# Attention and two expert stages on one core: the router's broadcast loads and the gated rows change their DMA queue

## Chip, core and metric

The kernel runs on 1 core of one Trainium2 chip. The metric is the device time of one execution in microseconds (us). The core has five engines that each run their own list of instructions in order: PE (matmul; its weight loads are listed apart as PEld), DVE (vector), ACT (scalar), POOL (GpSimd) and SP (sync), which here only issues DMAs. A DMA is issued by one engine's list and then moves data on 16 DMA engines that all lists share. An instruction that waits for a semaphore holds up what is behind it in its own list, and nothing else.

## The reference, cut to what matters

Three stages follow one another: attention in chunks, a dense expert with a clipped gate, and a mixture of 8 experts where each token goes to one expert.

```
for each chunk of 32 queries:                    # batch 4, heads 8, seq 768, head_dim 64
    k_full = [mem_k (8), k[chunk - 16 : chunk + 32 + 8]];  v_full likewise
    out = softmax(q_c @ k_full.T / 8) @ v_full
x = out as 3072 tokens x 512

h = x @ w_in                                     # 512 -> 2048
x = (h * clip(h + 3, 0, 6) / 6) @ w_out          # 2048 -> 512

xn = x / |x|;  en = expert_emb / |expert_emb|    # 8 experts
logits = xn @ en.T / tau
expert_idx = argmax(logits);  gate_w = softmax(logits)[expert_idx]
out[tokens of e] = gate_w * (relu(x @ w1[e]) @ w2[e])
```

## The kernel before

The 3072 tokens are 24 tiles of 128 tokens, in 8 blocks of 4, 2, 3, 3, 3, 3, 3 and 3 tiles. A loop over blocks `bl` does the dense expert of block `bl` and, woven in, the attention of the next block's tiles and the routing of block `bl - 1`. One loop has 16 steps `f`, one for each 128 columns of the hidden layer. In a step PE does `mm1(bl, f + 1)`, 12 matmuls to the hidden part `h` (L435); ACT and DVE make `g` from it (L450, L451) and split it into `gh` (ACT, L443) and `gl` (DVE, L446); `mm2(bl, f)` is 9 matmuls from gh and gl into `acc` (L491), two with gh ahead of one with gl for each of 3 tiles. Between the two matmul groups the step's list `slot[f]` is run: pieces of attention and routing.

Attention of one tile is six pieces in steps 5a to 5a + 5. The first, `st_t`, has DVE transpose k_t into the ring `kt` (L220) and q_t into qT (L258); `put_k` then copies borders of the ring with four or five small copies on POOL (L215, L224 to L231), which wait for the transpose on DVE. As soon as the transposes have read k_t and q_t, the next tile's loads go out on SP's queue: `load_blocks` (L145) issues 16 small loads for k_t and 16 for q_t. Piece 5 issues the loads of v (L179, and of mem_v, L189) on SP, which wait for PE to be done with the buffer (L334).

Routing of a block is done in two ways. Blocks 1 to 5 (`by_dots`) take dot products on DVE: `r_en` loads one expert's scaled embedding from the DRAM tensor `en_d`, one row of 2 KB to all 128 partitions, into `enb` (L577); `r_dot` multiplies it with a tile's x2 and sums (L583). `enb` has two buffers: `r_en(bl, 0)` and `r_en(bl, 1)` stand in slot 0, behind the first attention piece, and the load for expert e + 2 is issued behind the last tile's dot with expert e. The dots are spread over steps 1 to 10 by the numbers in `DOTS`; one of each step is put between gh and gl of `mm1`, so that `gl` stands behind it on DVE. These are the loops bl = 2 to 6, from about 226 to 737 us of the trace. At step 14 `r_gate` writes the block's rows, 512 values and the inverse of the gate's sum, to the DRAM tensor `xb` (L715), one DMA for each tile. The tile x2 is then free for the next evacuation of `acc` (`evac`, L508 on DVE and L510 on ACT, in the next loop behind its first mm1). Blocks 0, 6 and 7 are routed with matmuls and write their rows in the same `r_gate`.

After the loops the expert stage (from about 745 us on) gathers rows from xb with indirect DMAs on POOL (L802, tile `xg`) and scatters its results the same way.

The order on each engine's list is that of the program: the scheduler is off, and a DMA is in the list of the engine whose name it is called on. POOL's list holds, in these loops, the copies of put_k and one small power (`root`, L604) and no DMA.

Of the kernel before, what the change touches and what calls it, by code (L numbers as in the profile page):

```python
# [17 lines left out]
P = 128  # L18
# [13 lines left out]
def attn_moe_kernel(ctx, tc, q, k, v, mem_k, mem_v, w_in, w_out, emb, tau, w1, w2, out, dbg=None):  # L32
    nc = tc.nc
    B, H, S, D = q.shape
    M = mem_k.shape[2]
    NTOK, DM = out.shape
# [71 lines left out]
    xb = dram.tile([NTOK, XW], F32, name="xb")  # L108
# [406 lines left out]
    def small(shape, dt=F32, name="small", bufs=1):  # L515
        return sb.tile(shape, dt, tag=name, name=name, bufs=bufs)
# [49 lines left out]
    en_d = dram.tile([E, DM], F32, name="en_d")  # L566
    enb = {}

    def by_dots(bl):

        return 1 <= bl <= NB - 3

    def r_en(bl, e):

        if e < E:
            enb[bl, e] = sb.tile([P, DM], F32, tag="dec", name="enb", bufs=2)
            nc.sync.dma_start(out=enb[bl, e], in_=en_d[e:e + 1, :].to_broadcast([P, DM]))  # L577

    def r_dot(bl, t, e):
        if (t, e) == (0, 0):  # L580
            blk[bl] = (small([P, BS[bl]], name="ss"), small([P, BS[bl], E], name="lg"))
        x2 = x2_t[bl, t]
        V.scalar_tensor_tensor(  # L583
            out=x2[:, XW + 1:XW + 1 + DM // 2].bitcast(BF16), in0=x2[:, 0:DM], scalar=1.0, in1=enb[bl, e],
            op0=ALU.mult, op1=ALU.mult, accum_out=blk[bl][1][:, t, e:e + 1])
        if t == BS[bl] - 1:
            r_en(bl, e + 2)
# [109 lines left out]
    def r_gate(bl):  # L697

        lg, oh = blk[bl][1:3]
        TB = BS[bl]  # L700
        for t in range(TB if bl < NB - 1 else 0):
            V.tensor_tensor(out=ocum, in0=ocum, in1=oh[:, t, :], op=ALU.add)
        sm = small([P, TB], name="r_sm")
        V.tensor_reduce(out=sm, in_=lg, axis=AX.X, op=ALU.add)
        V.tensor_scalar(out=sm, in0=sm, scalar1=1e-9, scalar2=None, op0=ALU.add)
        if bl == 0:
            V.reciprocal(out=sm, in_=sm)
            nc.sync.dma_start(out=xb[0:TB * P, DM:XW].rearrange("(t p) o -> p (t o)", p=P), in_=sm)
        for t in range(TB):
            x2 = x2_t.pop((bl, t))  # L710
            r0 = (F0[bl] + t) * P
            if bl:
                V.reciprocal(out=x2[:, DM:DM + 1], in_=sm[:, t:t + 1])
            w = XW if bl else DM
            nc.sync.dma_start(out=xb[r0:r0 + P, 0:w], in_=x2[:, 0:w])  # L715

    cnt = const.tile([1, E], F32, name="cnt")

# [274 lines left out]
    with tc.manual_schedule():  # L993
# [149 lines left out]
        for bl in range(NB):  # L1143
# [10 lines left out]
            if by_dots(bl - 1):  # L1154
                for e in range(2):
                    slot.setdefault(0, []).append(lambda e=e: r_en(bl - 1, e))
                dots = [lambda t=t, e=e: r_dot(bl - 1, t, e) for e in range(E) for t in range(BS[bl - 1])]
                for f, n in enumerate(DOTS, 1):
                    mids[f], dots = dots[:1], dots[1:]
                    slot.setdefault(f, []).extend(dots[:n])  # L1160
                    dots = dots[n:]
                for t in range(BS[bl - 1]):
                    slot.setdefault(10 + t // 2, []).append(lambda t=t: r_ss(bl - 1, t))
                for f, r_ in ((10, r_route), (11, r_rank), (12, r_sel), (13, r_list), (14, r_exp), (14, r_gate)):
                    slot.setdefault(f, []).append(lambda r_=r_: r_(bl - 1))
            else:
                d = 2 if bl == 1 else 0
                for t in range(BS[bl - 1]):
                    (wt, f), (wl, f2) = (RT4 if bl == 1 else RT)[t], (RL4 if bl == 1 else RL)[t]
                    (pre_, slot)[wt].setdefault(f, []).append(lambda t=t: r_t(bl - 1, t, spare(bl)))  # L1170
                    (pre_, slot)[wl].setdefault(f2, []).insert(0, lambda t=t: r_l(bl - 1, t))
                    slot.setdefault((8, 8, 9, 9)[t] + d // 2, []).append(lambda t=t: r_ss(bl - 1, t))
                for f, r_ in ((8, r_route), (9, r_rank), (10, r_sel), (11, r_list), (12, r_exp), (12, r_gate)):
                    slot.setdefault(f + d, []).append(lambda r_=r_: r_(bl - 1))
# [98 lines left out]
        e_mm1(n1, s1, 0, [2, 3])  # L1273
        go(1, 3, 0, nc.gpsimd)
        r_gate(L)
        low()
        r_sel(L)
# [40 lines left out]
        with tc.If(tot > GS):  # L1318
            for s in range(GS, NS):
                with tc.If(tot > s):  # L1320
                    e = nc.values_load(reg["tab"][0:1, 0, s:s + 1], engines=[SP], min_val=0, max_val=E - 1)
# [42 lines left out]
```

## Time and profile before

| | us |
|---|---|
| median of 3 runs | 1160.51 |
| lowest, highest run | 1159.67, 1161.5 |
| profiled execution, its own time | 1163.16 |
| its span, first to last instruction | 1161.2 |
| PE busy | 1019.8 |
| DVE busy | 575.0 |
| ACT busy | 401.6 |
| POOL busy | 164.3 |

All times in the rows are us from the span's start, of this one execution. A row of the timeline gives start, length, engine (SPq is SP's DMA issues), line, operation, the written tile, what is read, and the count; brackets hold how long the engine was idle ahead of it and what ended that. PE's clock has two levels, 1.2 and 2.4 GHz; the mean granted clock of the span is 0.945 of the higher.

### The profile page before, as it was taken

Reading aid. Unit: us, or ns where it says so; the run is one execution under the profiler, and the core shown is the slowest. Engines: PE = TensorE matmul, PEld = TensorE weight load, DVE = VectorE, ACT = ScalarE, POOL = GpSimd, SP = SyncE. Lnnn points to the kernel's source line nnn. Section 1 sums busy time; section 2 is a strip of 40 time slices with the busy share of each in tenths; the row PEclk is TensorE's granted clock in tenths of the full one; section 3 lists DMA queues with packets and bytes.
Section 4 is the critical chain, followed back from the end, with each engine's and each line's share of the span. In section 5 each row is a group of like instructions: output and inputs, shape, how many; then the busy total and the mean of one; then the engine's idle time right before and its main releaser. Section 6 shows DMA issues by size and latency. Waiting matters only on the chain.

```text
span 1161.2 us, 22724 instructions
## 1 busy us (share of the span) xinstructions
PE 1019.8 (88%) x8006; PEld 853.2 (73%) x8006; DVE 575.0 (50%) x1357; ACT 401.6 (35%) x715; POOL 164.3 (14%) x210
## 2 busy tenths in 40 slices
PE   8798999947967895978689599999899999999996
PEld 5576787747856774866577488898688888888884
DVE  5687755535426643562455276466513442415631
ACT  5344434212212231232123123356324443525631
POOL 2134720000000000000000000003311112112111
PEclk9999999979997997989799899999899999999998
DMA  9755511322222222222232220433113532426520
GB/s 188 176 146 180 182 36 29 64 60 62 36 53 68 62 60 46 52 61 58 62 71 52 48 64 18 136 110 118 55 38 101 175 128 78 157 73 227 196 98 29
DMA packets 177629, 106.04 MB, mean 91 GB/s; under 512 B 139373, under 2 KB 147597, under 8 KB 177504
## 3 DMA queue, kind: packets, MB, share of 16 engines
q1 hardware_dynamic: 172864, 91.03, 29.2%
q0 software_dynamic: 4480, 13.44, 3.5%
q8 instruction: 65, 1.06, 0.4%
q14 instruction: 60, 0.49, 0.1%
q10 hardware_dynamic: 160, 0.02, 0.0%
HBM read 167.31 MB, written 13.40 MB: 156 GB/s over the span
## 4 chain that ended last, share of the span: by engine, by line
PE 56%; SPq 12%; DVE 11%; issue 8%; DMA 7%; ACT 4%; POOL 1%; DVEq 0%; POOLq 0%; ACTq 0%
PE h L435 14%; PE acc L491 14%; PE acc L865 10%; SPq L145 10%; PE h L834 10%; DMA enb<-en_d 3%; DMA xb<-x 2%; PE s L843 2%; ACT g L450 1%; DVE g L451 1%; ACT gh L443 1%; PE s L334 1%; DMA out_dram<-r,m_tid 1%; DVE gl L446 1%; PE att L816 1%
## 5 line engine op out<-in xcount | busy, mean ns | idle before, releaser
L491 PE MATMUL acc<-wo,gh 128*128 128x512 f32 x640 | 218.5, 424 | 6.0 <-DVE x L508 3.6
L491 PE MATMUL acc<-wo,gl 128*128 128x512 f32 x320 | 135.6, 424 | 78.9 <-DVE gl L446 78.9
L435 PE MATMUL h<-xh,w_in_h 128*128 128x384 f32 (+2 forms) x512 | 178.7, 349 | 5.7 <-DVE wo L473 2.4
L435 PE MATMUL h<-xl,w_in_h 128*128 128x384 f32 (+2 forms) x512 | 176.6, 345 | 0.7 <-DVE xl L371 0.6
L435 PE MATMUL h<-xh,w_in_l 128*128 128x384 f32 (+2 forms) x512 | 175.2, 342 | 0.0
L450 ACT ACTIVATE g<-h,three 128x384 f32<-128x384 f32 (+1 forms) x112 | 63.2, 565 | 231.5 <-PE h L435 207.5
L491 PEld LDWEIGHTS acc<-wo,gh 128*128 128x128 f32 x640 | 119.6, 199 | 31.7 <-DVE x L508 5.2
L491 PEld LDWEIGHTS acc<-wo,gl 128*128 128x128 f32 x320 | 64.5, 201 | 97.7 <-DVE gl L446 82.9
L583 DVE SCALAR_TENSOR_TENSOR x<-x,enb 128x512 bf16<-128x512 f32 x112 | 74.6, 681 | 116.6 <-DMA enb<-en_d 116.6
L451 DVE SCALAR_TENSOR_TENSOR g<-g,h 128x384 f32<-128x384 f32 (+1 forms) x112 | 59.8, 534 | 137.5 <-ACT g L450 137.1
L435 PEld LDWEIGHTS h<-xh,w_in_h 128*128 128x128 f32 x512 | 100.1, 195 | 15.6 <-DVE wo L473 3.9
L435 PEld LDWEIGHTS h<-xl,w_in_h 128*128 128x128 f32 x512 | 99.6, 195 | 9.4 <-DVE xl L371 2.0
L435 PEld LDWEIGHTS h<-xh,w_in_l 128*128 128x128 f32 x512 | 99.1, 194 | 3.0
L443 ACT CAST gh<-g 128x384 fp32r<-128x384 f32 (+1 forms) x112 | 55.8, 498 | 85.5 <-DVE g L451 85.5
L446 DVE TENSOR_TENSOR gl<-g,gh 128x384 fp32r<-128x384 f32 (+1 forms) x112 | 60.8, 543 | 35.4 <-ACT gh L443 35.4
L224 POOL COPY kt<-kt 128x192 f32<-128x192 f32 x15 | 5.2, 346 | 487.5 <-DVE kt L220 487.5
L821 DVE TENSOR_TENSOR tl<-att,th 128x512 fp32r<-128x512 f32 x26 | 18.0, 691 | 112.7 <-ACT th L820 106.6
L802 POOL DMA_INDIRECT xg<-xb,m_ix x27 | 27.8, 1031 | 257.9 <-PE h L834 211.8
L865 PE MATMUL acc<-wo,th 128*128 128x512 f32 x192 | 60.6, 397 | 0.0
L296 ACT ACTIVATE e<-e 128x512 f32<-128x512 f32 x20 | 12.6, 632 | 124.5 <-DVE e L293 124.5
L837 ACT ACTIVATE hs<-h 128x512 f32<-128x512 f32 x54 | 32.1, 598 | 64.4 <-PE h L834 60.5
L820 ACT CAST th<-att 128x512 fp32r<-128x512 f32 x26 | 15.2, 586 | 106.0 <-PE acc L865 104.3
(324 smaller groups left out, 1841.1 us busy)
## 6 DMA issues: line engine op xcount, KB each, us to landing
rw<-in_moe_w_dram SPq DMA_DIRECT2D x136, 512.0 KB
enb<-en_d SPq DMA_DIRECT2D x40, 256.0 KB
vw<-in_v_dram SPq DMA_DIRECT2D x176, 56.0 KB
raw_in<-in_moe_w_in_dram SPq DMA_DIRECT2D x16, 512.0 KB
raw_out<-in_moe_w_out_dram SPq DMA_DIRECT2D x16, 512.0 KB
xb<-x SPq DMA_DIRECT2D x20, 256.5 KB
k_t<-in_k_dram SPq DMA_DIRECT2D x240, 16.0 KB
q_t<-in_q_dram SPq DMA_DIRECT2D x240, 16.0 KB
```

Of the source, the lines that this page charges most:

```text
L145: nc.sync.dma_start(out=t[g:g + 32].rearrange("p h d -> p (h d)").rearrange("p (j c d) -> p j c d", j=4, c=NCH)[:, :, c, :], in_=x[b, r::2 ...
L435: nc.tensor.matmul(hp, lhsT=wt[:, c, f * P:(f + 1) * P], rhs=xc, start=(n == 0), stop=(n == 3 * KD - 1))
L443: nc.scalar.copy(out=gh, in_=g)
L446: nc.vector.tensor_tensor(out=gl, in0=g, in1=gh.bitcast(F32), op=ALU.subtract)
L450: nc.scalar.activation(out=g, in_=hp, func=AF.Relu, bias=three)
L451: nc.vector.scalar_tensor_tensor(out=g, in0=g, scalar=6.0, in1=hp, op0=ALU.min, op1=ALU.mult)
L491: nc.tensor.matmul(acc[bl][t], lhsT=gt[:, t * P:(t + 1) * P], rhs=wo[hl, f // 2][:, f % 2, :], start=(f == first and n == 0), stop=(f == l ...
L583: V.scalar_tensor_tensor(out=x2[:, XW + 1:XW + 1 + DM // 2].bitcast(BF16), in0=x2[:, 0:DM], scalar=1.0, in1=enb[bl, e], op0=ALU.mult, op1= ...
L802: nc.gpsimd.indirect_dma_start(out=t[:, :], out_offset=None, in_=src, in_offset=bass.IndirectOffsetOnAxis(ap=ix[:, 0:1], axis=0), bounds_c ...
L834: nc.tensor.matmul(hp, lhsT=a[:, kk, :], rhs=wpart(st, hl, p, kk), start=(kk == 0 and a is th and hl == 0), stop=(kk == KD - 1 and a is tl))
L837: nc.scalar.activation(out=h_t[n][:, p, :], in_=hp_t.pop((n, p)), func=AF.Relu)
L865: nc.tensor.matmul(o, lhsT=a[:, KD + f, :], rhs=wpart(st, hl, 2 + half, kk), start=(f == 0 and c == 0), stop=(f == KE - 1 and c == 2))
```

## The change

Two calls change the engine on which they are made. The embeddings' loads `enb` (8 for each of 5 blocks, 40 in all) are issued by POOL instead of SP, and so are the writes of x2's rows to xb for the blocks that are routed by dots (14 of the 24). What is transferred, into which buffers and after which instructions stays the same.

```
-            nc.sync.dma_start(out=enb[bl, e], in_=en_d[e:e + 1, :].to_broadcast([P, DM]))
+            nc.gpsimd.dma_start(out=enb[bl, e], in_=en_d[e:e + 1, :].to_broadcast([P, DM]))
...
-            nc.sync.dma_start(out=xb[r0:r0 + P, 0:w], in_=x2[:, 0:w])
+            (nc.gpsimd if by_dots(bl) else nc.sync).dma_start(out=xb[r0:r0 + P, 0:w], in_=x2[:, 0:w])
```

The lists of PE, DVE and ACT stay as they are. SP's list in the loop bl = 5 (542 to 645 us) before, where `enb` stands for the embeddings, `vw` for v's window and `xb` for the rows:

```order
L145 DMA k_t<-in_k_dram 32x4x32 x16
L145 DMA q_t<-in_q_dram 32x4x32 x16
L577 DMA enb<-en_d 128x512 x4
L179 DMA vw_95<-in_v_dram 56x4x64 x8
L577 DMA enb<-en_d 128x512
...
L577 DMA enb<-en_d 128x512 x3
L179 DMA vw_96<-in_v_dram 56x4x64 x8
...
L715 DMA xb<-x_5901 128x513
```

The same list with the change:

```order
L145 DMA k_t<-in_k_dram 32x4x32 x16
L145 DMA q_t<-in_q_dram 32x4x32 x16
L179 DMA vw_95<-in_v_dram 56x4x64 x8
...
L179 DMA vw_96<-in_v_dram 56x4x64 x8
```

Only the loads of k_t, q_t and v are left there.

POOL's list from the end of loop bl = 5 through loop bl = 6, before (L604 is the power of the norms):

```order
L604 TENSOR_TENSOR rn_y_6667<-ss,half 128x3
L224 COPY kt<-kt 128x4x3x16
L227 COPY kt<-kt 128x4x16
L228 COPY kt<-kt 128x4x3x8
L231 COPY kt<-kt 128x4x8
L224 COPY kt<-kt 128x4x3x16
L228 COPY kt<-kt 128x4x3x8
L231 COPY kt<-kt 128x4x8
L604 TENSOR_TENSOR rn_y_7613<-ss,half 128x3
```

And with the change, from the last row of xb on:

```order
L715 DMA xb<-x_5905 128x513
L224 COPY kt<-kt 128x4x3x16
L227 COPY kt<-kt 128x4x16
L228 COPY kt<-kt 128x4x3x8
L231 COPY kt<-kt 128x4x8
L577 DMA enb<-en_d 128x512 x5
L224 COPY kt<-kt 128x4x3x16
L228 COPY kt<-kt 128x4x3x8
L231 COPY kt<-kt 128x4x8
L577 DMA enb<-en_d 128x512 x3
L604 TENSOR_TENSOR rn_y_7613<-ss,half 128x3
```

The first enb of a loop stands behind the copies of the first attention piece, five go out ahead of the second piece's copies and three behind them; the xb writes stand behind the power and ahead of the next loop's first copies.

## Rows read from the trace of the kernel before

**Rows 1.** The page: the chain that ended last, shares of the span by engine

```profile
PE 56%; SPq 12%; DVE 11%; issue 8%; DMA 7%; ACT 4%; POOL 1%; DVEq 0%; POOLq 0%; ACTq 0%
```

**Rows 2.** Waits of the whole span: us in total, times, longest

```profile
DVE x L583 <- DMA enb<-en_d: 116.6, 9, 17.9
PE acc L491 <- DVE gl L446: 78.9, 8, 14.5
```

**Rows 3.** Timeline of SP's issues, loop bl = 5

```profile
542.96 7.45 SPq L145 DMA_DIRECT2D k_t<-in_k_dram  x16
550.51 7.66 SPq L145 DMA_DIRECT2D q_t<-in_q_dram  x16
558.22 14.54 SPq L577 DMA_DIRECT2D enb<-en_d  x4
...
582.21 7.44 SPq L145 DMA_DIRECT2D k_t<-in_k_dram  x16
589.75 8.47 SPq L145 DMA_DIRECT2D q_t<-in_q_dram  x16
```

**Rows 4.** Timeline of DVE, the same loop

```profile
543.86 0.55 DVE L451 SCALAR_TENSOR_TENSOR g<-g,h 128x384 f32<-128x384 f32 x1 [0.33 <-ACT g L450]
561.70 0.69 DVE L583 SCALAR_TENSOR_TENSOR x<-x,enb 128x512 bf16<-128x512 f32 x1 [17.29 <-DMA enb<-en_d]
562.32 0.55 DVE L446 TENSOR_TENSOR gl<-g,gh 128x384 fp32r<-128x384 f32 x1
...
601.65 0.69 DVE L583 SCALAR_TENSOR_TENSOR x<-x,enb 128x512 bf16<-128x512 f32 x1 [7.29 <-DMA enb<-en_d]
```

**Rows 5.** Timeline of PE: the first stall of loop 5, the second of loop 2

```profile
562.93 0.79 PE L491 MATMUL acc<-wo,gl 128*128 128x512 f32 x1 [13.36 <-DVE gl L446]
...
289.33 1.18 PE L334 MATMUL s<-vw,pT 64*32 64x64 f32 x64 [5.86 <-ACT pT L322]
```

**Rows 6.** The chain in order of time: start, us, what; behind both stalls of loop 5

```profile
562.93 3.35 PE acc L491 x7
566.28 3.17 PE h L435 x12
...
569.89 2.08 PE acc L491 x9
571.97 2.09 PE h L435 x12
...
602.88 3.33 PE acc L491 x7
```

**Rows 7.** Timeline of POOL: the last of loop 5's first border copies

```profile
543.74 0.21 POOL L231 COPY kt<-kt 128x32 f32<-128x32 f32 x1
```

**Rows 8.** Line 802, the gathers on POOL: ns shortest/median/longest, and landing

```profile
L802 POOL DMA_INDIRECT xg<-xb,m_ix x27: 1006/1023/1194, 740.7 to 1121.4; - x27
...
DMA to landing us min/median/max: 3.3/3.5/7.6
```

**Rows 9.** Line 189, the four plain loads that POOL issues at the start

```profile
DMA to landing us min/median/max: 3.4/3.8/4.3
```

**Rows 10.** Timelines at three loop ends: reciprocals, row writes, evacuations, PE behind them

```profile
530.81 0.29 DVE L713 RECIPROCAL x<-r_sm 128x1 f32<-128x1 f32 x3
533.70 1.31 SPq L715 DMA_DIRECT2D xb<-x  x3
537.32 0.73 PE L491 MATMUL acc<-wo,gh 128*128 128x512 f32 x2 [0.93 <-ACT x L510]
538.94 0.73 PE L491 MATMUL acc<-wo,gh 128*128 128x512 f32 x2 [0.65 <-DVE x L508]
...
330.70 0.73 PE L491 MATMUL acc<-wo,gh 128*128 128x512 f32 x2 [1.35 <-DVE x L508]
...
642.44 0.60 ACT L510 ACTIVATE x<-acc 128x512 f32<-128x512 f32 x1 [0.29 <-DMA xb<-x]
```

**Rows 11.** Busy time by stretch: us, PE, PEld, DVE, ACT, POOL, PEclk, DMA, GB/s

```profile
745.00:800.00 55.00, 55.00 (x327) 49.21 (x326) 34.44 (x78) 30.29 (x51) 5.81 (x3) 1.00 0.39 129
```

## The prediction

> **What bounds the kernel now.** I began with the page. PE is busy 1019.8 of 1161.2 us, yet the chain that ended last gives PE only 56% and SP's queue 12% [rows 1]: for over a tenth of the time the end hangs on the issuing of DMAs. The waits say where. DVE stands 116.6 us, in only 9 pieces, before the dot products of L583 until a broadcast embedding lands, and PE stands 78.9 us in 8 pieces before the second matmuls (L491) until DVE delivers gl [rows 2]. 9 long waits are one pattern, so I read one loop, from 542 to 645 us.
>
> There SP issues 16 loads of k_t and 16 of q_t, one after another, and only then the first enb: 542.96 to 558.17 us go by on 32 small issues [rows 3]. DVE had done its transposes at 543 and could take the first dot at 544.4; it starts it at 561.70, and gl, which stands behind the dot on DVE, at 562.32 [rows 4]. PE waits for this gl until 562.93, 13.36 us, so it wanted it at 549.57 [rows 5]. The same comes a second time in the loop: q_t's issues end at 598.22, only then can the three last enb go out, and DVE's dot starts at 601.65, 7.29 us late [rows 3, 4]. All five dot loops (226 to 737 us) have the first stall, the first four the second. In the first loop the second stall is put down to ACT (5.86 us at 289.33), because DVE's wait there holds g and through it ACT's copies [rows 5].
>
> **What the change does to the enb stalls.** It takes 40 enb issues and 14 xb issues from SP; nothing is added on DVE, PE or ACT, whose order stays. On GpSimd the first two enb of a loop stand behind the copies of put_k, which end at 543.95 in this loop [rows 7]; from there, not from 558, their time counts. Then:
> - Removed idle of PE: 78.9 + 5.86 = 84.8 us [rows 2, 5]. All 8 waits of the first number are the two enb places.
> - Removed slow clock. After these stalls PE's rows are stretched: 7 matmuls of L491 take 3.35 us and 12 of L435 3.17, where a little later 9 take 2.08 (7 would be 1.62) and 12 take 2.09 [rows 6]. That is 1.73 + 1.08 = 2.8 us behind a first stall and, by the row at 602.88, 3.33 - 1.62 = 1.7 behind a second. I take 5 x 2.8 + 4 x 1.75 = 21.0 us. That PE may run at full clock without these pauses is shown by 745 to 800 us: busy 55 of 55 us, granted clock 1.00 [rows 11].
>
> **What takes their place.** No DMA of this form, 128 rows of 2 KB issued by GpSimd, is in the trace. The nearest by size and rows is the gather xg, 128 rows of 2 KB: 1.02 us on GpSimd, 3.3/3.5/7.6 us from issue to landing (shortest, median, longest) [rows 8]. The nearest by kind are the four small plain loads of L189 on GpSimd, 3.4/3.8/4.3 us [rows 9]. From SP an enb takes 561.70 - 558.22 = 3.5 us until its dot starts [rows 3, 4]. PE wants gl at 549.57, and from dot start to PE's matmul 562.93 - 561.70 = 1.23 us pass; so the first enb may land as late as 548.3, that is 4.4 us behind the copies. The medians, 3.5 and 3.8, leave no wait of PE, although DVE itself still stands some 3 us. The longest of the plain loads, 4.3, with 0.3 us to start, would overrun by 0.3 to 0.4. I take 0.36 x 5 = 1.8 us: the upper end of the nearest kind. Bounds: 0, and with 7.6 us 3.5 us of idle plus some 1.7 of slow clock in each loop, 26 us.
>
> The later enb: two buffers, so enb e+2 goes out when the last dot of e is done. Three tiles' dots are spread at two or three for each step of about 4.6 us, which by my estimate from the order of the dots and their 0.69 us [rows 4] leaves 3.5 us in the tightest place and 4 to 10 elsewhere; the 1.0 us of descriptor work is inside the 3.5 us to landing. Cost 0, cover: DVE's own slack in each step. Copies of put_k behind an enb on GpSimd would have to wait while that enb waits for a dot; but the transpose on DVE which they need stands behind the same dot, so only the 1.02 us of issue can be added, and the order has it done a step before. Cost 0, at most 1 us in a few places.
>
> What is late next? k_t and q_t. From one transpose to the next five steps pass: SP's k_t issues start at 542.96 and 582.21, 39.25 us, less the stall and its clock (16.2) 23.1 us [rows 3, 5, 6]. The 32 issues take 15.2 and a load lands some 3.5 later: 18.7, so 4 us are to spare, less where v's loads stand ahead. Cost 0.
>
> What the skill says against it: by the Trainium skill, "DMA: Bandwidth & Descriptors", section "Issuing engines are not separate DMA queues", several issuing engines save only the sequencer's issue time, usually small beside the DMA. The trace agrees with the first half; the second half does not hold here, where 15.2 us of issue stand before 3.5 us of DMA.
>
> **What the change does to xb.** Three writes per loop (two in the first) go out at the loop's end, and the next evacuation needs their tiles. In two loops SP is late, behind loads of v: the reciprocal is done at 531.1, the writes start at 533.70, and PE idles 0.93 us and then 0.65 between evacuations; in the first loop 1.35 us [rows 10]. GpSimd is free there. That gives back some 1.6 + 1.3 = 2.9 us. In the other three the writes start at once, and the last evacuation waits 0.29 us [rows 10]. On GpSimd starts lie 1.02 us apart [rows 8], so the third goes out 2 us behind the first and lands 3.5 later, 5.5 us in all, about as now. Cost 0; with 7.6 us about 3 us in each of five loops.
>
> **The sum**, against the profiled execution: 1163.2 us (span 1161.2 and 2.0 around it) - 84.8 - 21.0 - 2.9 + 1.8 = 1056.3. It was 2.65 us above the median of 1160.51, so the forecast on the runs' scale is 1053.6.
>
> **Rivals.**
> (A) Landings on GpSimd as slow as its slowest row, 7.6 us. The first stall comes back with 26 us in all instead of 1.8. The tight later enb overrun too, by up to 4 us of DVE against about 1.7 us of slack a step: 0 to 20 us more. Time 1078 to 1098. For it: its DMA engines are shared with the small k_t packets. Against: the 7.6 is one extreme beside weight loads of 512 KB, and both medians are under 4. Chance 0.08.
> (B) SP's wait is only an issue cost: the loads behind it and DVE's own work hold PE anyway, so that only the 54 moved issues of about 0.36 us count, 19 us. Time 1141, or no change if those are hidden too. Against: DVE's rows name the landing, and between the two stalls PE runs step on step without a wait. The page on DMA quoted above would lead one here. Chance 0.05, of which 0.02 no change.
> (C) Slower: GpSimd's descriptors are held up by DVE's work, so that every enb lands late, in the ring of two. Four turns then stand in a row, each a landing and three dots of 0.69 us: the sixth dot group (e = 5) starts at 543.95 + 3L + 4.1 for a landing time L. It stands at 601.65 now, so at L of about 17.9 us this place is where it was. The fourth turn (e = 7) is quick now: 601.65 + 2 us of dots + 3.5 of landing = 607.2. With 543.95 + 4L + 6.2 the kernel is slower from about L = 14 us; at 20 us the turn ends at 630.2, 23 us late, x 5 loops = 115, time 1275. The longest landing in the trace, 7.6, is far from it, and the 27 gathers issued beside a working DVE took 1.006 to 1.194 us [rows 8]. Chance 0.03. The rule behind it is in the Trainium skill, "SBUF — State Buffer", section "SBUF: two separate sides": while VectorE runs an operation in a two-port mode GpSimd can't write descriptors. The gathers' even durations show little of that here; whether a plain broadcast load suffers more no run shows yet.
>
> **How the numbers follow.** Forecast 0.84, A 0.08, B 0.05, C 0.03. The forecast's own range is 1045 to 1070: below, the second stalls' clock is larger in one loop and small waits go with the big ones; above, 1 to 3 us in each loop at the first enb. To hold 8 in 10 with A's lower part I take 1044 to 1080. A measurement of this kernel tells about 0.2% from no change. Faster 0.95, same 0.02, slower 0.03.
>
> **What would show it.** Right: DVE's wait for enb falls from 116.6 to some 15 to 20 us, in five pieces of about 3 to 4; PE's wait for gl nearly vanishes; a loop shrinks from 103 to about 81 to 83 us; SP's rows are gone from between; the expert part from 745 on keeps its length. Wrong: enb landing over 4.4 us behind its issue, PE waiting in the loop for q_t or s, evacuations waiting longer for xb, or dots longer than 0.69 us beside GpSimd's descriptor work.

## The result, and the profile after

The changed kernel takes 1058.28 us (median of 4 runs, 1055.30 to 1061.04), the kernel before in the same comparison 1160.09 us (1158.36 to 1161.50): a ratio of 0.912, 95% interval 0.909 to 0.915. Forecast were 1053.6 us, in a range from 1044 to 1080. The profiled execution took 1057.8 us, its span 1056.0.

The first fence is from the page of the changed kernel and its waits: the chain by engine, the group of matmuls that waited for gl (busy time, mean ns, then idle time and what ended it), and two waits (us in total, times, longest).

```profile
PE 68%; DVE 11%; issue 7%; DMA 6%; ACT 4%; POOL 2%; SPq 2%; DVEq 0%; POOLq 0%; ACTq 0%
...
L491 PE MATMUL acc<-wo,gl 128*128 128x512 f32 x320 | 127.6, 399 | 0.4 <-DVE gl L446 0.4
...
DVE x L583 <- DMA enb<-en_d: 17.5, 10, 3.8
...
PE att L678 <- ACT pT L322: 9.9, 5, 2.0
```

SP's queue has fallen from 12% of the chain to 2% [rows 1]. DVE still waits for embeddings, 17.5 us instead of 116.6, but TensorE's wait for gl is 0.4 us instead of 78.9 [rows 2]: DVE's remaining waits are covered. The largest wait of TensorE inside the dot loops is now another one, for ScalarE's copy of pT. It was there before too, with 10.0 us in five pieces, beside longer ones.

Loop bl = 5, which begins at 470.6 us here, shows how. The fence has the rows of SP, of GpSimd, of DVE and of TensorE from the timelines of the changed kernel (start, duration, engine and line).

```profile
470.64 7.63 SPq L145 DMA_DIRECT2D k_t<-in_k_dram  x16
478.38 8.13 SPq L145 DMA_DIRECT2D q_t<-in_q_dram  x16
...
471.42 0.21 POOL L231 COPY kt<-kt 128x32 f32<-128x32 f32 x1
471.57 1.10 POOL L577 DMA_DIRECT2D enb<-en_d  x2
...
475.56 0.69 DVE L583 SCALAR_TENSOR_TENSOR x<-x,enb 128x512 bf16<-128x512 f32 x1 [2.73 <-DMA enb<-en_d]
476.18 0.55 DVE L446 TENSOR_TENSOR gl<-g,gh 128x384 fp32r<-128x384 f32 x1
...
477.12 0.39 PE L491 MATMUL acc<-wo,gl 128*128 128x512 f32 x1
```

SP still issues its 32 small loads, until 486.5, but the first embedding goes out right behind the copies of put_k and is there at 475.56, 4.0 us after its issue began, while those loads are being issued. The dot that waited 17.29 us [rows 4] waits 2.73, and the matmul behind gl starts without a wait, where it stood 13.36 us [rows 5]. From the first k_t load of this loop to that of the next 81.8 us pass instead of 102.9.

All five dot loops together, from windows over them (the stretch, its length, busy us of PE, PEld, DVE, ACT and POOL with instructions, PE's granted clock, DMA share, GB/s); first the kernel before, then the changed one:

```profile
226.00:739.50 513.50, 411.44 (x3792) 355.86 (x3790) 255.71 (x711) 124.34 (x246) 17.03 (x62) 0.90 0.24 55
```

```profile
226.00:629.00 403.00, 387.33 (x3793) 338.53 (x3793) 256.07 (x712) 124.62 (x246) 47.28 (x116) 0.99 0.32 70
```

They are 110.5 us shorter. TensorE's idle time there falls from 513.50 - 411.44 = 102.1 us to 15.7, that is by 86.4, and its busy time for the same matmuls by 24.1, as the granted clock rises from 0.90 to 0.99. The span shrank by 105.2 us only. The missing 5.3 us lie at the very end. The next two fences show it, before and then after: ScalarE's last operation (range of starts), and two of GpSimd's instructions in the code that ends the kernel, INC_SWDGE_SEM and DRAIN (ns shortest, median, longest, then first and last start).

```profile
L871 ACT ACTIVATE r<-acc,m_gate x27: 687/694/694, 836.1 to 1149.9; 128x512 f32<-128x512 f32 x27
...
L1318 POOLq INC_SWDGE_SEM  x1: 1371/1371/1371, 1154.1 to 1154.1; - x1
...
L1359 POOLq DRAIN  x3: 51/103/4882, 1155.5 to 1161.0; - x3
```

```profile
L871 ACT ACTIVATE r<-acc,m_gate x27: 687/694/695, 725.5 to 1039.2; 128x512 f32<-128x512 f32 x27
...
L1318 POOLq INC_SWDGE_SEM  x1: 2447/2447/2447, 1043.4 to 1043.4; - x1
...
L1359 POOLq DRAIN  x3: 46/103/9292, 1045.9 to 1055.7; - x3
```

ScalarE's last operation starts 110.7 us earlier, but from there to the end of the span it takes 1056.0 - 1039.2 = 16.8 us instead of 11.3, and GpSimd's longest DRAIN lasts 9.29 us instead of 4.88, INC_SWDGE_SEM 2.45 instead of 1.37. The change adds 54 DMAs to GpSimd's list. Whether that is the cause is tested below.

### The profile page after: what moved, and what is told of

Read it like the earlier page. It is cut to its first block, busy times and chain, and to the rows that moved or that the text cites. A ratio compares the mean times of both kernels' runs of the same rounds, so it can differ in the third digit from the quotient of the medians.

```text
span 1056.0 us, 22770 instructions
## 1 busy us (share of the span) xinstructions
PE 997.5 (94%) x8006; PEld 836.3 (79%) x8006; DVE 575.1 (54%) x1357; ACT 401.6 (38%) x715; POOL 196.1 (19%) x264
## 4 chain that ended last, share of the span: by engine, by line
PE 68%; DVE 11%; issue 7%; DMA 6%; ACT 4%; POOL 2%; SPq 2%; DVEq 0%; POOLq 0%; ACTq 0%
PE h L435 18%; PE acc L491 18%; PE acc L865 11%; PE h L834 11%; DMA xb<-x 2%; PE s L843 2%; DVE g L451 1%; PE s L276 1%; ACT gh L443 1%; ACT g L450 1%; DMA out_dram<-r,m_tid 1%; PE att L816 1%; PE s L334 1%; DVE gl L446 1%; DVE dec L413 1%
## 5 line engine op out<-in xcount | busy, mean ns | idle before, releaser
L491 PE MATMUL acc<-wo,gh 128*128 128x512 f32 x640 | 209.4, 409 | 5.0 <-ACT x L510 3.3
L435 PE MATMUL h<-xh,w_in_h 128*128 128x384 f32 (+2 forms) x512 | 175.1, 342 | 4.2 <-DVE wo L473 2.4
L435 PE MATMUL h<-xl,w_in_h 128*128 128x384 f32 (+2 forms) x512 | 173.5, 339 | 0.7 <-DVE xl L371 0.5
L491 PEld LDWEIGHTS acc<-wo,gh 128*128 128x128 f32 x640 | 113.5, 190 | 29.2 <-ACT x L510 7.1
L491 PE MATMUL acc<-wo,gl 128*128 128x512 f32 x320 | 127.6, 399 | 0.4 <-DVE gl L446 0.4
L435 PEld LDWEIGHTS h<-xh,w_in_h 128*128 128x128 f32 x512 | 96.9, 189 | 14.0 <-DVE wo L473 3.9
L435 PEld LDWEIGHTS h<-xl,w_in_h 128*128 128x128 f32 x512 | 96.9, 189 | 8.9 <-DVE xl L371 1.9
L583 DVE SCALAR_TENSOR_TENSOR x<-x,enb 128x512 bf16<-128x512 f32 x112 | 75.0, 680 | 17.5 <-DMA enb<-en_d 17.5
L491 PEld LDWEIGHTS acc<-wo,gl 128*128 128x128 f32 x320 | 60.7, 190 | 15.3 <-DVE gl L446 1.4
L820 ACT CAST th<-att 128x512 fp32r<-128x512 f32 x26 | 15.2, 586 | 107.4 <-PE acc L865 105.6
L865 PE MATMUL acc<-w_in_h,th 128*128 128x512 f32 x120 | 49.3, 411 | 0.0
L834 PE MATMUL h<-wo,th 128*128 128x512 f32 x192 | 48.9, 397 | 0.0
```

The costliest lines, as they stand in the source:

```text
L435: nc.tensor.matmul(hp, lhsT=wt[:, c, f * P:(f + 1) * P], rhs=xc, start=(n == 0), stop=(n == 3 * KD - 1))
L491: nc.tensor.matmul(acc[bl][t], lhsT=gt[:, t * P:(t + 1) * P], rhs=wo[hl, f // 2][:, f % 2, :], start=(f == first and n == 0), stop=(f == l ...
L583: V.scalar_tensor_tensor(out=x2[:, XW + 1:XW + 1 + DM // 2].bitcast(BF16), in0=x2[:, 0:DM], scalar=1.0, in1=enb[bl, e], op0=ALU.mult, op1= ...
L834: nc.tensor.matmul(hp, lhsT=a[:, kk, :], rhs=wpart(st, hl, p, kk), start=(kk == 0 and a is th and hl == 0), stop=(kk == KD - 1 and a is tl))
L865: nc.tensor.matmul(o, lhsT=a[:, KD + f, :], rhs=wpart(st, hl, 2 + half, kk), start=(f == 0 and c == 0), stop=(f == KE - 1 and c == 2))
```

## The experiments

Two theories about the gain stood against each other: that TensorE had waited for embeddings which SP's list held back (the prediction), and that the issues themselves cost the time (rival B). Two more questions came from the result: what the 5.5 us at the end are, and what bounds the loops now.

### Only the embeddings moved

The changed kernel with the rows of x2 back on SP:

```diff
-            (nc.gpsimd if by_dots(bl) else nc.sync).dma_start(out=xb[r0:r0 + P, 0:w], in_=x2[:, 0:w])
+            nc.sync.dma_start(out=xb[r0:r0 + P, 0:w], in_=x2[:, 0:w])
```

> Only the 40 embedding loads move to GpSimd; the 14 writes of gated rows stay on SP. Theory (the loads stood on SP behind 32 small issues of k_t and q_t, and this alone holds DVE and through it PE): nearly the whole gain, 1060 to 1066 us, since the writes were worth 2.9 us in the forecast; DVE's wait for enb near 17.5 us as with both moves; at two loop ends evacuations wait longer for xb. Rival 1 (only the cost of issuing counts, 40 x 0.36 us): 1146 us. Rival 2 (the writes carry a good part of the gain): over 1080 us.

Measured: 1057.78 us (1056.86 to 1059.29), ratio 0.912 (0.908 to 0.916). The whole gain is here. Its profile, the waits:

```profile
DVE x L583 <- DMA enb<-en_d: 14.8, 8, 3.5
...
PE acc L491 <- DVE x L508: 2.9, 3, 1.3
```

TensorE's waits for the evacuations of `acc`, a part of which the prediction charged to SP's late xb writes, are 2.9 us for DVE's and 1.7 for ScalarE's in this run. In the changed kernel they are 1.6 and 3.3, and in the kernel before 3.6 and 2.3: with the rows moved as well, the wait shifts from one engine's evacuations to the other's, and its sum does not fall (4.6 here, 4.9 there). ScalarE's last operation starts 0.8 us later in this run than in the changed kernel, and its end is 1.5 us shorter.

### Only the rows of x2 moved

The kernel before with the other line of the diff alone.

> Only the 14 writes of gated rows move to GpSimd; the embedding loads stay on SP. Theory: 1160.1 - 2.9 = 1157 us (1154 to 1160), DVE's wait for enb stays at some 117 us in 9 pieces. Rival 2 (the writes carry a good part of the gain): 1140 us or less.

Measured: 1155.66 us (1153.18 to 1159.10, 10 runs), ratio 0.996 (0.994 to 0.998): a small gain, within the range expected, but not shown to come from where it was expected. In the profiles ScalarE's last operation starts 5.2 us earlier than in the kernel before, yet TensorE's idle time in the dot loops is only 1.3 us less and its waits for evacuations 0.4 us less (5.5 instead of 5.9); the other 3.9 us are shorter busy time for the same matmuls, and what shortens it stays open. The gain does not add to the other: with the embeddings gone from SP, nothing is left of it (previous run).

### The first two embeddings ahead on SP's own list

The kernel before; two of eight embeddings of a loop are issued ahead of the loads of k_t and q_t, still by SP:

```diff
-                    slot.setdefault(0, []).append(lambda e=e: r_en(bl - 1, e))
+                    slot.setdefault(0, []).insert(e, lambda e=e: r_en(bl - 1, e))
```

> The kernel before with one edit: the first two embedding loads of each loop are issued on SP ahead of the loop's first k_t and q_t loads instead of behind them. The same queue, the same number of issues; only their order on SP changes. Theory (place in the queue, not engine and not issue cost): the first stall of each loop goes, but the third load (e = 2) now stands behind the same 32 issues: these end some 15.5 us after the transposes, the load lands 3.5 later, about 3 us after its dot could start, of which 1.7 is covered by DVE's slack, so about 1.5 us of PE idle a loop remain there; the second stall stays. 1160.1 - (67.4 + 14) + 7.5 = 1086 us, 1080 to 1096. Rival 1 (issue cost on SP): no change, 1160 us. Rival 3 (the loads are slow because the DMA engines are busy with k_t and q_t, whoever issues them): the first loads still land late, since they now run beside those, over 1120 us.

Measured: 1105.48 us (1101.84 to 1107.66), ratio 0.952 (0.948 to 0.957). Half of the gain comes without any other engine, but less than the 1080 to 1096 us expected. Its timelines of SP, DVE and PE in one loop:

```profile
406.86 1.10 SPq L577 DMA_DIRECT2D enb<-en_d  x2
416.04 8.51 SPq L145 DMA_DIRECT2D k_t<-in_k_dram  x16
424.65 7.50 SPq L145 DMA_DIRECT2D q_t<-in_q_dram  x16
432.24 0.85 SPq L577 DMA_DIRECT2D enb<-en_d  x2
...
417.42 0.68 DVE L583 SCALAR_TENSOR_TENSOR x<-x,enb 128x512 bf16<-128x512 f32 x1
...
435.61 0.69 DVE L583 SCALAR_TENSOR_TENSOR x<-x,enb 128x512 bf16<-128x512 f32 x1 [6.29 <-DMA enb<-en_d]
...
438.57 0.66 PE L204 MATMUL att<-ident,xo 128*128 128x128 f32 x4 [2.44 <-DVE xo L341]
```

The first dot, at 417.42, has no wait at all. Its embedding was issued at 406.86, 9 us ahead of the first small load, so this run does not test whether the small loads slow an embedding down by what they move (rival 3 of the expectation). The changed kernel does: there the first embedding of a loop goes out while SP issues the 32 loads, and no embedding takes longer than 5.6 us to land. But the third embedding needs a buffer that the first dots free, so it still stands behind q_t's issues, and its dot, for which DVE was free at 429.32, waits until 435.61. I had taken 3 us for that wait; it is 6.29, and all of DVE's waits for embeddings in this run sum to 61.6 us. The larger part of the shortfall is the clock. In the loops TensorE's idle time falls by 54.4 us (102.1 to 47.7) where 60 were expected, but its busy time only by 4.1 us where 14 were: in four of the five loops the new wait, 2.2 to 4.6 us long, is still followed by a low clock, as after the one of 2.44 us above, behind which the granted clock from 438.6 to 443.0 us is 0.61. So a place further ahead in one list helps only as far as the buffers reach; a list that is not blocked, as in the changed kernel, helped every embedding.

### The embeddings on ScalarE's list

The changed kernel, with ScalarE in GpSimd's place for the embeddings (the rows of x2 stay on GpSimd):

```diff
-            nc.gpsimd.dma_start(out=enb[bl, e], in_=en_d[e:e + 1, :].to_broadcast([P, DM]))
+            nc.scalar.dma_start(out=enb[bl, e], in_=en_d[e:e + 1, :].to_broadcast([P, DM]))
```

> As the changed kernel, but the 40 embedding loads are issued from ACT's list; the writes stay on GpSimd. Theory (any list that is not full of other loads will do): the long waits are gone as well; what is new is that a load on ACT waits there for DVE's last dot with the buffer, and ACT's next g and gh stand behind it. DVE has some 1.7 us of slack a step, so small new waits in some steps: 1060 to 1085 us, 1068 as the single figure. Rival (GpSimd is special, for instance because its descriptors pass the SP ring of small loads): the long waits come back, over 1120 us.

Measured: 1053.25 us (1052.63 to 1056.42), ratio 0.907 (0.904 to 0.911), better than expected. From its trace, the issues (ns shortest, median, longest) and ScalarE's wait for the landing of an embedding:

```profile
L577 ACTq DMA_DIRECT2D enb<-en_d x40: 326/327/444, 226.7 to 590.8; - x40
...
ACT g L450 <- DMA enb<-en_d: 6.9, 3, 2.4
```

I had thought that the issues would hold up ScalarE's own work. 40 x 0.33 us of issue and three short waits do not: ScalarE is busy 401.6 us, 38% of the span, in the changed kernel. GpSimd is nothing special, then: ScalarE's list does as well. By the profiles this run is up to ScalarE's last operation 2.2 us later than the changed kernel (1041.4 against 1039.2), and its end is 4.0 us shorter. By the medians it is 5.0 us faster; its profiled execution took 1056.4 us where its median is 1053.25, so the 2.2 us are not to be relied on.

### A dose of delay for the first embeddings

The prediction allowed the first embedding to land 4.4 us behind put_k's copies. Here the changed kernel gets four small GpSimd operations between those copies and the first two embeddings, in each loop:

```diff
+        for _ in range(4):
+            nc.gpsimd.tensor_tensor(out=pad, in0=half, in1=half, op=ALU.pow)
```

> The changed kernel with four small GpSimd operations (128x4 power, some 1.05 us each by the nearest row, about 4.2 us in all; their results are not used) put between put_k's copies and the first two embedding loads of each of the five loops: a dose of delay for the loads alone. The prediction said that the first load may land up to 4.4 us after put_k's copies before TensorE waits. In the changed kernel VectorE's first dot of a loop waits 2.4 to 3.8 us for its embedding, and TensorE waits 0.4 us in all on the matmuls behind it. Theory (the window is that narrow, 4.4 us or a little more): VectorE's first dots wait some 4 us more each, TensorE waits 2 to 4 us per loop with 1.7 to 2.8 us of low clock behind, five loops, 1076 to 1092 us. Rival (VectorE has more slack ahead of TensorE than the prediction worked out): VectorE waits 4 us more per loop, TensorE hardly any, 1057 to 1063 us.

Measured: 1082.96 us (1079.96 to 1086.77), ratio 0.935 (0.932 to 0.938). Its timelines of GpSimd, DVE and PE in the last dot loop:

```profile
569.78 0.20 POOL L231 COPY kt<-kt 128x32 f32<-128x32 f32 x1
569.96 4.29 POOL L584 TENSOR_TENSOR pad<-half 128x4 f32<-128x4 f32 x4
574.20 1.15 POOL L577 DMA_DIRECT2D enb<-en_d  x2
...
578.19 0.69 DVE L590 SCALAR_TENSOR_TENSOR x<-x,enb 128x512 bf16<-128x512 f32 x1 [6.87 <-DMA enb<-en_d]
...
579.42 0.80 PE L491 MATMUL acc<-wo,gl 128*128 128x512 f32 x1 [3.70 <-DVE gl L446]
```

4.29 us of delay turn into 3.70 us of TensorE's idle time, and in the five loops into 18.6. The copies end at 569.98 and the dot starts 8.2 us behind; 8.2 less the allowed 4.4 is 3.8. The changed kernel fits the same window: its one wait for gl, 0.35 us at 314.56, is in the loop where the first dot starts latest behind the copies, 313.33 - 308.58 = 4.75 us. So the window is as narrow as it was worked out to be. The low clock behind these stalls is smaller than expected: for the matmuls of the five loops TensorE is busy 391.3 us, 3.9 more than in the changed kernel, or 0.8 us per loop, not the 1.7 to 2.8 that I expected. The granted clock of the whole span is 0.981 in this execution and 0.976 to 0.979 in the other three, so there it may be more.

### 54 tiny DMAs on GpSimd in the kernel before

The end of the kernel grew. Is it the number of DMAs on GpSimd, or what they move? The kernel before gets 54 DMAs of 4 bytes each, in a stretch of the last loop in which GpSimd is idle:

```diff
+        for i in range(54):
+            nc.gpsimd.dma_start(out=pad[i:i + 1, :], in_=tau.unsqueeze(0))
```

> The kernel before with 54 GpSimd DMAs of 4 bytes each added in the last loop, where GpSimd is idle (work that is not in the computation). The change adds 54 DMAs of 128 rows each to GpSimd's queue, and the kernel's end, from ScalarE's last operation on, grew from 11.3 to 16.8 us with GpSimd's DRAIN at the end 4.88 us before and 9.29 us after. Theory (this price is per DMA issued on GpSimd, whatever its size): DRAIN 9.3 us, INC_SWDGE_SEM 2.4 us, the time 1160.4 + 5.4 = 1166 us (1163 to 1169). Rival (it is per row or per byte that the DMA moves): DRAIN stays within 0.3 us of 4.9 us, the time within 2 us of 1160.

Measured: 1166.05 us (1164.23 to 1169.70), ratio 1.006 (1.003 to 1.008). The same two lines of its trace as above (in this kernel they stand under other numbers):

```profile
L878 ACT ACTIVATE r<-acc,m_gate x27: 688/694/694, 836.3 to 1151.4; 128x512 f32<-128x512 f32 x27
...
L1367 POOLq DRAIN  x3: 50/103/9297, 1157.9 to 1167.7; - x3
```

DRAIN takes 9.30 us as in the changed kernel, though the DMAs move 4 bytes instead of 256 KB, and from ScalarE's last operation to the end of the span 16.6 us pass. The price is one for each DMA that GpSimd has issued. The other kernels lie on the same line: 14 more than before (only the rows moved) give 6.03 us, 40 (only the embeddings) 8.15, 54 (both) 9.29, which is 0.082 us each.

### r_list one slot later

The waits for pT, 9.9 us in five pieces, are TensorE's largest in the loops of the changed kernel. r_list's matmul (L678) writes the bank that pT is copied from; one slot later the copy is long done:

```diff
-                for f, r_ in ((10, r_route), (11, r_rank), (12, r_sel), (13, r_list), (14, r_exp), (14, r_gate)):
+                for f, r_ in ((10, r_route), (11, r_rank), (12, r_sel), (14, r_list), (14, r_exp), (14, r_gate)):
```

> The changed kernel with one edit: r_list, which ends the router's part of a loop, stands in slot 14 instead of slot 13. In the changed kernel TensorE's largest remaining wait of each loop is the router's matmul of r_list, 1.85 to 2.05 us (five times, at 288.61, 369.25, 449.22, 531.68 and 612.96) for ScalarE's copy of pT out of the bank that both use, and a stretch at the low clock follows it in four loops. Theory (these waits bound the loops now, and a wait costs itself plus what the low clock takes behind it): five waits of 2.0 us and some 1.7 us of low clock behind each go, 5 x 3.7 = 18 us, so about 1040 us (1036 to 1048). Rival (the wait is only handed on: DVE's stages are late next, or the low clock falls somewhere else anyway): within 4 us of 1058.

Measured: 1040.91 us (1039.35 to 1043.31), ratio 0.897 (0.895 to 0.899), 17.4 us below the changed kernel by the medians and 14.5 by the spans of the two profiles. Its dot loops, by windows (columns as above):

```profile
226.00:615.00 389.00, 383.25 (x3797) 336.96 (x3798) 256.56 (x713) 125.83 (x248) 47.13 (x116) 1.00 0.34 73
```

TensorE's idle time falls from 15.7 to 5.75 us, by 9.9, just the five waits, and its busy time by 4.1. The clock's part was expected at 8.5: in the profiled execution of the changed kernel only two of the five waits are followed by a stretch at the low clock, not four as I had read. The medians, 17.4 us apart, are close to the 18 expected; whether in other executions more of the five waits are followed by a low clock, no trace shows. The windows of the changed kernel over these two:

```profile
451.00:455.00 4.00, 4.00 (x15) 3.51 (x15) 0.00 (x0) 0.00 (x0) 0.00 (x0) 0.62 0.09 14
533.00:537.00 4.00, 4.00 (x14) 3.32 (x14) 0.00 (x0) 0.00 (x0) 0.00 (x0) 0.63 0.14 21
```

### Both lessons at once

The embeddings on ScalarE, the rows of x2 on SP, r_list in slot 14:

```diff
+            nc.scalar.dma_start(out=enb[bl, e], in_=en_d[e:e + 1, :].to_broadcast([P, DM]))
+            nc.sync.dma_start(out=xb[r0:r0 + P, 0:w], in_=x2[:, 0:w])
+                for f, r_ in ((10, r_route), (11, r_rank), (12, r_sel), (14, r_list), (14, r_exp), (14, r_gate)):
```

> The changed kernel with three edits: the embedding loads are issued on ScalarE instead of GpSimd, the rows of x2 go back to SP, and r_list stands in slot 14. If the three act apart: 1053.3 measured with the loads on ScalarE, less 18 us for r_list's waits (the same five waits as in the run with r_list alone), less some 1.4 us of the kernel's end for the 14 DMAs that GpSimd no longer issues: about 1034 us (1028 to 1043). If r_list's waits are only handed on: 1050 to 1054.

Measured: 1040.68 us (1039.17 to 1040.87), ratio 0.897 (0.895 to 0.899): as fast as the run before, not 7 us faster. The DRAIN is back at 4.88 us, as expected, and the waits for pT are gone. But ScalarE's last operation starts at 1027.9, 3.1 us later than with r_list alone, and DVE's evacuations make TensorE wait 4.2 us instead of 1.9:

```profile
PE acc L491 <- DVE x L508: 4.2, 3, 2.1
...
L1359 POOLq DRAIN  x3: 51/103/4882, 1033.2 to 1038.7; - x3
```

By the profiles the step from the embeddings on ScalarE to here is 1041.4 - 1027.9 = 13.5 us at ScalarE's last operation, against 14.4 for r_list alone; with the end it is 15.3 us, by the medians 12.6. The 18 us in my sum were the two theories' full price; what of the shortfall is scatter between executions, and what is xb's return to SP, stays open. This kernel and the one with r_list alone are the fastest, 10% below the kernel before.

## Why the prediction held, step by step

| step | predicted | measured in the profiles |
|---|---|---|
| TensorE's idle time in the dot loops | -84.8 - 2.9 + 1.8 = -85.9 us | -86.4 us |
| slow clock behind the stalls | -21.0 us | -24.1 us |
| the end, behind ScalarE's last operation | 0 | +5.5 us |
| profiled time | 1056.3 us | 1057.8 us |

The idle time agrees as a sum. Of its parts the two waits behind embeddings, 84.8 us, are gone but for 0.35 us, which is what the first embeddings cost instead of 1.8; xb gave less than the 2.9 put down for it (the waits for evacuations fell from 5.9 to 4.9 us).

- **What the embeddings waited for.** Right: SP's list, not the DMAs. The stall went when the issue moved to GpSimd, to ScalarE, and for the first dot when it moved ahead on SP. Rival B, that only issue costs count, is refuted by the embeddings alone: 40 issues moved and 102 us gone.
- **What the skill says.** By the Trainium skill, "DMA: Bandwidth & Descriptors", section "Issuing engines are not separate DMA queues", another issuing engine saves only the sequencer's time, usually small. That the saving is issue time agrees with the run in which the first dot had no wait on SP's own list; that it is small does not hold here, where 15.2 us of issue stood ahead of an embedding [rows 3] and moving the embeddings alone gave 102 us.
- **The first embedding.** The window of 4.4 us was right, by the dose; the residue was 0.35 us instead of 1.8. DVE's waits of 2.4 to 3.8 us in five pieces, plus short later ones, sum to 17.5 us, inside the 15 to 20 forecast.
- **GpSimd's price.** Mis-sized: taken from the gathers, 1.02 us for an issue; it is 0.55 us. Embeddings land 3.4/3.7/5.6 us after their issue (shortest, median, longest), so rival A's 7.6 did not come, and TensorE waited for one first embedding only. The fence has the issue row of the changed kernel and its landing.

```profile
L577 POOL DMA_DIRECT2D enb<-en_d x40: 546/546/663, 229.3 to 590.4; - x40
...
DMA to landing us min/median/max: 3.4/3.7/5.6
```

- **Rival C** needed landings of 14 us and more; the longest is 5.6. The 40 issues last 0.546 us with hardly an exception and 0.663 at most, though DVE is busy for 256 of the 403 us of these loops. The rule weighed there, in the Trainium skill, "SBUF — State Buffer", section "SBUF: two separate sides", that VectorE's two-port operations keep GpSimd from writing descriptors, shows no price in this kernel. Whether a VectorE operation beside these issues ran in such a mode, no run here shows.
- **xb.** Mis-sized: 2.9 us expected, at most 0.8 found on top of the embeddings, and its 14 DMAs lengthen the end by 1.5 us, which is more. Moved alone, with the embeddings still on SP, it gave 4.7 us by the medians and 1.3 us of idle time, so that gain is not explained by these waits. The landing was taken as 3.5 us; on GpSimd it is 5.0 (the page's median). The longer landing fits the longer waits of ScalarE's evacuations, but no run took it alone.

```profile
xb<-x POOLq DMA_DIRECT2D x14, 256.5 KB, 5.0
```

- **What is late next.** Right that k_t and q_t are not. Missed: the waits for pT, 2 us in each loop. They stood in the profile of before with the same total and were counted in neither kernel, so the forecast did not suffer; but they were worth 14.5 us by the profiles and 17.4 by the medians.
- **The expert part.** What stands behind the dot loops, the dense expert's last loop and the 8 experts, kept its length up to ScalarE's last operation (410.4 us before, 410.2 after); the end of the kernel did not. This is the one term of the sum that was missing: the prediction put nothing down for what a DMA on GpSimd costs at the kernel's end. On the profile's scale the forecast is 1.5 us off (1057.8 against 1056.3): 5.5 us of the end, less 3.1 us that the clock gave back beyond the forecast, and under a us of idle time. That it comes so close is in part luck, since the two larger errors offset each other. On the scale of the runs it is 4.7 us off, since I took 2.65 us off for a profile above the median, and the profile of the changed kernel lies 0.5 us below its own.

## What to carry to other kernels

Ask of a DMA that lands late not only how long it takes but what stands ahead of it in the list of the engine that issues it: 32 issues of half a us each held TensorE up for 13.4 us in a loop of 103. Here another free list, GpSimd's or ScalarE's, cured that for every load, a better place in the same list only as far as the buffers reached. And a wait of the bound engine is worth its length plus a part at the low clock that must be read behind each such wait, since it followed some of them and not others, and here it followed waits of 2.4 us as well as waits of 13.

## What the runs showed of the hardware

- Each DMA that GpSimd issues lengthens the end of the kernel: DRAIN by 0.082 us, from 4.88 us before to 9.29 with 54 more, and INC_SWDGE_SEM there by 0.020 us, from 1.37 to 2.45. It holds for 4 bytes as for 256 KB, and not for DMAs that ScalarE issues. For n DMAs that is 0.1 us x n in this kernel, to be set against what the move gains.
- A DMA of 128 rows of 2 KB occupies GpSimd for 0.546 us, ScalarE's list for 0.327 us.
